# Attention with a KV cache and a gMLP branch on one core: picking heads by one product, a four-tile last wo group, and w_out's rest in 14, 10 and 8 rows

## The chip, the cores and the metric

The kernel runs on one core of one Trainium2 chip. The metric is the time of one run on the device in microseconds; I quote medians of several runs. In the profile PE is TensorE (PEld its weight loads), DVE is VectorE, ACT ScalarE, POOL GpSimd and SP SyncE; L458 is line 458 of the kernel concerned. The granted clock is the speed that TensorE was allowed, 1.00 being full speed. A load has landed when its last byte has arrived.

## The reference

Four tokens, one per batch, with 32 heads of 128 and caches of 4096 positions; the result has the shape (4, 1, 640).

```python
def reference(A_x, A_k_cache, A_v_cache, A_wq, A_wo, B_x, B_w_in, B_w_sp, B_b_sp, B_w_out):
    def _A_ref(x, k_cache, v_cache, wq, wo):      # B, Sq, D = 4, 1, 640; H, Dh = 32, 128
        q = (x @ wq).reshape(B, Sq, H, Dh).transpose(0, 2, 1, 3)
        scores = einsum('bhqd,bhkd->bhqk', q, k_cache) * Dh ** (-0.5)
        o = einsum('bhqk,bhkd->bhqd', softmax(scores), v_cache)
        return o.transpose(0, 2, 1, 3).reshape(B, Sq, H * Dh) @ wo
    def _B_ref(x, w_in, w_sp, b_sp, w_out):       # w_out: 864 x 640
        ...                                       # gelu, layernorm, gate, product with w_out
    xn = _layernorm(A_x)
    return A_x + _A_ref(xn, A_k_cache, A_v_cache, A_wq, A_wo) + _B_ref(xn, B_w_in, B_w_sp, B_b_sp, B_w_out)
```

## The kernel before

The caches are almost all of the 282.25 MB that are loaded. The heads are treated in four groups of eight (`NG = 4`, `HG = 8`), each in four units of K and of V, one per batch. A unit of V gives O (128 partitions x 4 x 128) in PSUM; four masked VectorE instructions make `R[:, b]` of it. When the four batches of a group are there, `emit_sel` picks each head's row (into `om`), `emit_oT` turns the result (into `oT`), and `emit_proj` multiplies it by the group's rows of wo. `o_bf` is the final sum, which is stored. Only for the last group is nothing left to load behind which this could be done.

```python
    # early: the last 96 rows of w_out, as 32 partitions of 3 rows (3840 bytes each), between w_out and K
    w_rest_d = B_w_out[nf:Fh, :].rearrange("(i r c) n -> r i c n", r=4, c=FR)
    for r in range(4):
        nc.sync.dma_start(out=w_rest[r:32:4], in_=w_rest_d[r])
    ...
    def emit_sel(g):
        oh = misc_ps([G, Dh], F32)                      # G = 32 rows: 8 heads x 4 batches
        for b in range(B):
            nc.tensor.matmul(oh[:], lhsT=SelR[:, b].rearrange("p h b -> p (h b)"), rhs=state["R"][:, b, :],
                             start=(b == 0), stop=(b == B - 1))
        om = ppool.tile([G, HG, Dh], BF16, tag="p", name="om")
        nc.vector.scalar_tensor_tensor(out=om[:], in0=oh[:, None, :].to_broadcast((G, HG, Dh)), ...)
    ...
    emit_proj(NG - 3)                                   # the tail, after V's last unit
    emit_sel(NG - 1)
    emit_proj(NG - 2, range(0, 4))
    emit_oT(NG - 1)
    emit_proj(NG - 2, range(4, HG))

    o_1 = ppool.tile([64, NO2], F32, tag="p", name="o_1")
    nc.vector.tensor_tensor(out=o_1[:], in0=proj[0:64, 0:NO2], in1=x_res[:], op=ALU.add)
    nc.vector.tensor_tensor(out=o_1[:], in0=proj[64:128, 0:NO2], in1=o_1[:], op=ALU.add)
    last = ps_l.tile([64, NO2], F32)
    oT = state[("oT", NG - 1)]
    for c in range(HG):
        lhsT = oT[:].rearrange("p c b -> p (c b)") if c == 0 else oT[:, c, :]
        for hf in range(NH):                            # two column tiles
            nc.tensor.matmul(last[32 * hf:32 * hf + (32 if c == 0 else B), :], lhsT=lhsT,
                             rhs=wo_t[NG - 1][:, c, hf * NO2:(hf + 1) * NO2], start=(c == 0), stop=(c == HG - 1))
    o_bf = ppool.tile([64, NO2], BF16, tag="p", name="o_bf")
    nc.vector.tensor_tensor(out=o_bf[:], in0=last[:], in1=o_1[:], op=ALU.add)
```

Of the kernel before, what the change touches and what calls it, by code (L numbers as in the profile page):

```python
# [9 lines left out]
ALU = mybir.AluOpType  # L10
AX = mybir.AxisListType
F32 = mybir.dt.float32
BF16 = mybir.dt.bfloat16
# [3 lines left out]
def kernel(  # L17
# [19 lines left out]
    nc = tc.nc  # L37
    P = 128
    B, Sq, D = A_x.shape
    _, H, Sk, Dh = A_k_cache.shape  # L40
    assert Sq == 1 and B == 4 and Dh == P and D % P == 0
    DC = D // P
    HG = 8
# [8 lines left out]
    NG = H // HG  # L52
    NU = NG * B
    G = HG * B
    F2 = B_w_in.shape[1]
    Fh = F2 // 2
    FA = 6
    FR = (Fh - FA * P) // 32
# [4 lines left out]
    NO2 = NOUT // NH  # L63
# [3 lines left out]
    const = ctx.enter_context(tc.tile_pool(name="const", bufs=1))  # L67
    small = ctx.enter_context(tc.tile_pool(name="small", bufs=2))
# [8 lines left out]
    ps_l = ctx.enter_context(tc.tile_pool(name="ps_l", bufs=1, space=bass.MemoryType.PSUM))  # L77
# [3 lines left out]
    def misc_ps(shape, dtype):  # L81
        misc_ctr[0] += 1
        return ps_m.tile(shape, dtype, tag="misc", name=f"misc{misc_ctr[0]}")
# [5 lines left out]
    def at_slot(i, n, off=0):  # L89
        return kv[:, i * SL + off:i * SL + off + n]  # L90
# [24 lines left out]
    nf = FA * P  # L115
# [3 lines left out]
    w_rest = w_rest_t[:32].bitcast(BF16)[:, 0:FR * NOUT].rearrange("p (c n) -> p c n", c=FR)  # L119

    NB = 32 * FC
    z_at = n_in + FA * NOUT
    w_rest_d = B_w_out[nf:Fh, :].rearrange("(i r c) n -> r i c n", r=4, c=FR)
    for r in range(4):
        nc.sync.dma_start(out=w_rest[r:32:4], in_=w_rest_d[r])  # L125


    seq = [("k", u) for u in range(B)]
# [36 lines left out]
    wo_t = [at_slot((4, 0, 1, 2)[g], HG * NOUT).rearrange("p (c n) -> p c n", c=HG) for g in range(NG)]  # L165
# [61 lines left out]
    SelH = const.tile([P, HG], F32)  # L227
    nc.vector.tensor_reduce(out=SelH[:], in_=I32[:].rearrange("p (h c) -> p h c", c=4), axis=AX.X, op=ALU.add)
    Mk4 = const.tile([P, 4], F32)
    nc.vector.tensor_reduce(out=Mk4[:], in_=I32[:].rearrange("p (h c) -> p c h", c=4), axis=AX.X, op=ALU.add)  # L230
    SelR = const.tile([P, B, HG, B], F32)
    nc.gpsimd.memset(SelR[:].rearrange("p x h b -> p (x h b)"), 0.0)
    for b in range(B):
        nc.vector.tensor_copy(out=SelR[:, b, :, b], in_=SelH[:])

    MkE = const.tile([P, NE], F32)
    nc.vector.tensor_reduce(out=MkE[:], in_=I32[:].rearrange("p (e m) -> p e m", e=NE), axis=AX.X, op=ALU.add)
# [8 lines left out]
    B32f = const.tile([G, B], F32)  # L246
# [17 lines left out]
    for hf in range(2):  # L264
        for c in range(DC):
            for j in range(NG):
                n0 = j * HG * Dh + hf * 512
                nc.tensor.matmul(q4_ps[32 * j:32 * j + 32, hf * 512:hf * 512 + 512], lhsT=xnT[:, c, :],  # L268
                                 rhs=wq[:, c, n0:n0 + 512], start=(c == 0), stop=(c == DC - 1))
# [4 lines left out]
    for a in range(2):  # L274
        op = nc.vector.tensor_copy if a == 0 else nc.scalar.copy
# [13 lines left out]
    for c in range(DC):  # L289
        for q in range(4):  # L290
# [29 lines left out]
                                   op0=ALU.mult, op1=ALU.subtract)  # L320
# [14 lines left out]
    for fc in range(FC):  # L335
        n = P if fc < FA else 32
        nb = B if fc > 1 else 32
        r0 = 64 * (fc % 2)
        for hf in range(NH):
            nc.tensor.matmul(proj[r0 + 32 * hf:r0 + 32 * hf + nb, 0:NO2], lhsT=uT[:n, fc, 0:nb],  # L340
                             rhs=(w_out[:, fc] if fc < FA else w_rest[:, fc - FA])[:, hf * NO2:(hf + 1) * NO2], start=(fc < 2), stop=False)
# [9 lines left out]
    state = {}  # L351
# [104 lines left out]

    def emit_sel(g):

        oh = misc_ps([G, Dh], F32)
        for b in range(B):  # L460
            nc.tensor.matmul(oh[:], lhsT=SelR[:, b].rearrange("p h b -> p (h b)"), rhs=state["R"][:, b, :],  # L461
                             start=(b == 0), stop=(b == B - 1))
        om = ppool.tile([G, HG, Dh], BF16, tag="p", name="om")
        nc.vector.scalar_tensor_tensor(out=om[:], in0=oh[:, None, :].to_broadcast((G, HG, Dh)),  # L464
                                       scalar=state.pop(("rinv", g))[:, 0:1],
                                       in1=MkH[:, :, None].to_broadcast((G, HG, Dh)), op0=ALU.mult, op1=ALU.mult)
        state[("om", g)] = om

    def emit_oT(g):
        om = state.pop(("om", g))[:].rearrange("p h (q c) -> p c h q", c=HG)  # L470
        oT_ps = misc_ps([P, HG, B], F32)
        for c in range(HG):
            nc.tensor.matmul(oT_ps[:, c, :], lhsT=om[:, c, :, :], rhs=B32[:], start=True, stop=True)
        oT = small.tile([P, HG, B], BF16, tag="oT", bufs=3)
        nc.vector.tensor_copy(out=oT[:], in_=oT_ps[:])
        state[("oT", g)] = oT

    def emit_proj(g, cs=range(HG)):
# [9 lines left out]
    for i, item in enumerate(seq):  # L488
# [13 lines left out]
        g, b = divmod(u, B)  # L502
        if key == "k":
            done = b == B - 1 and g > 0
            for k in range(8):
                emit_K(u, k)
                if done and k == 1:
                    emit_sel(g - 1)
                if done and k == 2:
                    emit_oT(g - 1)  # L510
                if done and k == 5 and g == 1:
                    emit_proj(g - 1)
            if b == B - 1:
                if g < NG - 1:
                    fill_qz(g + 1)
                softmax(g)
        else:
            emit_V(u)
    emit_proj(NG - 3)
# [5 lines that stand above are left out]
    o_1 = ppool.tile([64, NO2], F32, tag="p", name="o_1")  # L525
    nc.vector.tensor_tensor(out=o_1[:], in0=proj[0:64, 0:NO2], in1=x_res[:], op=ALU.add)
    nc.vector.tensor_tensor(out=o_1[:], in0=proj[64:128, 0:NO2], in1=o_1[:], op=ALU.add)
    last = ps_l.tile([64, NO2], F32)
    oT = state[("oT", NG - 1)]
    for c in range(HG):  # L530

        lhsT = oT[:].rearrange("p c b -> p (c b)") if c == 0 else oT[:, c, :]
        for hf in range(NH):
            nc.tensor.matmul(last[32 * hf:32 * hf + (32 if c == 0 else B), :], lhsT=lhsT,  # L534
                             rhs=wo_t[NG - 1][:, c, hf * NO2:(hf + 1) * NO2], start=(c == 0), stop=(c == HG - 1))

    o_bf = ppool.tile([64, NO2], BF16, tag="p", name="o_bf")
    nc.vector.tensor_tensor(out=o_bf[:], in0=last[:], in1=o_1[:], op=ALU.add)
    nc.sync.dma_start(out=out_flat[:, 0:NO2], in_=o_bf[0:B, :])
    nc.scalar.dma_start(out=out_flat[:, NO2:NOUT], in_=o_bf[32:32 + B, :])  # L540
# [28 lines left out]
```

## Time and profile before

| | before |
|---|---|
| median of the first three runs | 664.79 us (664.62 to 665.85) |
| span of the profiled run | 663.0 us |
| V's last unit landed, first and second part | 645.02, 649.92 |
| R of the last batch complete | 653.18 |
| oT of the last group cast | 655.89 |
| last wo group landed, first and last of four pieces | 657.63, 659.25 |
| o_bf done, output stored until | 660.54, 663.0 |

Read the table from its last row upwards. The output needs o_bf, o_bf needs the last wo group's products, and these need two things: oT, which descends from R, and the pieces of wo. The prediction below shows the chain of waits and the timeline from which the rows come. The view by stretches gives start, end and length of a stretch in us, then the busy time and count of PE, PEld, DVE, ACT and POOL, then the granted clock, the DMA share and GB/s. In the kernel before, for the last products and the final sums:

```profile
657.70:660.60 2.90, 2.27 (x16) 1.07 (x15) 0.71 (x2) 0.00 (x0) 0.00 (x0) 0.51 0.07 26
```

The clock was at half speed there (0.51), the DMA engines had nearly nothing left to do (0.07), and VectorE executed two instructions.

### The profile page before, as it was taken

Reading aid. Unit: us, or ns where it says so; the run is one execution under the profiler, and the core shown is the slowest. Engines: PE = TensorE matmul, PEld = TensorE weight load, DVE = VectorE, ACT = ScalarE, POOL = GpSimd, SP = SyncE. Lnnn points to the kernel's source line nnn. Section 1 sums busy time; section 2 is a strip of 40 time slices with the busy share of each in tenths; the row PEclk is TensorE's granted clock in tenths of the full one; section 3 lists DMA queues with packets and bytes.
Section 4 is the critical chain, followed back from the end, with each engine's and each line's share of the span. In section 5 each row is a group of like instructions: output and inputs, shape, how many; then the busy total and the mean of one; then the engine's idle time right before and its main releaser. Section 6 shows DMA issues by size and latency. Waiting matters only on the chain.

```text
span 663.0 us, 5426 instructions
## 1 busy us (share of the span) xinstructions
PE 289.5 (44%) x2283; PEld 106.4 (16%) x2283; DVE 362.0 (55%) x339; ACT 79.5 (12%) x163; POOL 10.7 (2%) x34
## 2 busy tenths in 40 slices
PE   0525765166072455235436075433506244634245
PEld 0101221022021122111112022110202112111112
DVE  4338999656190749609255286745619084960002
ACT  1200000541100000530200000070100000053200
POOL 3000000000000000000000000000000000000000
PEclk9758779678577677767858577865958769767677
DMA  9999999999999999999999999999999999999996
GB/s 370 463 440 428 407 438 441 439 428 436 428 435 432 431 415 446 431 435 436 427 439 436 427 416 446 437 439 428 415 440 439 436 439 406 453 420 433 429 416 253
DMA packets 6901, 282.61 MB, mean 426 GB/s; under 512 B 808, under 2 KB 1084, under 8 KB 1500
## 3 DMA queue, kind: packets, MB, share of 16 engines
q1 hardware_dynamic: 6856, 282.25, 98.8%
q8 instruction: 18, 0.29, 0.2%
q14 instruction: 7, 0.06, 0.0%
q10 hardware_dynamic: 20, 0.01, 0.0%
HBM read 282.25 MB, written 0.01 MB: 426 GB/s over the span
## 4 chain that ended last, share of the span: by engine, by line
DMA 74%; DVE 11%; issue 11%; PE 2%; ACT 1%; SPq 0%; DVEq 0%; ACTq 0%
DMA kv<-in_A_k_cache_dram 64%; DVE kT L361 11%; DMA kv<-in_A_v_cache_dram 4%; DMA kv<-in_A_wo_dram 3%; DMA kv<-in_A_wq_dram 2%; PE O L444 2%; ACT xd L426 0%; ACT Zb L407 0%; PE last L534 0%; PE S L372 0%; ACT p L415 0%; DVE pT L419 0%; DVE m L379 0%; PE misc L384 0%; SPq L125 0%
## 5 line engine op out<-in xcount | busy, mean ns | idle before, releaser
L361 DVE STREAM_TRANSPOSE kT<-kv 128x2048 f32<-128x2048 f32 x128 | 282.8, 2276 | 132.1 <-DMA kv<-in_A_k_cache_dram 132.1
L372 PE MATMUL S<-kT,QZ 128*32 128x512 bf16 x1024 | 188.3, 500 | 239.0 <-DVE kT L361 239.0
L372 PEld LDWEIGHTS <-QZ 128*32 128x32 bf16 x1024 | 60.6, 111 | 361.5 <-issue 341.0
L444 PE MATMUL O<-kv,Zb 128*32 128x512 bf16 x1024 | 74.6, 457 | 57.0 <-DMA kv<-in_A_v_cache_dram 36.7
L451 DVE TENSOR_SCALAR R<-O,Mk 128x128 f32<-128x128 f32 x16 | 5.6, 351 | 120.5 <-PE O L444 120.5
L407 ACT ACTIVATE Zb<-xd,MkE 32x256 bf16<-32x256 bf16 x116 | 53.0, 498 | 108.9 <-PE O L444 107.5
L444 PEld LDWEIGHTS <-Zb 128*32 128x32 bf16 x1024 | 33.4, 112 | 97.0 <-issue 55.7
L415 ACT ACTIVATE p<-S,negmax 128x512 bf16<-128x512 f32 x8 | 5.4, 683 | 312.3 <-DVE negmax L393 312.3
L461 PE MATMUL misc<-R,SelR 128*32 128x128 f32 x32 | 6.4, 281 | 26.2 <-DVE R L453 26.2
L453 DVE SCALAR_TENSOR_TENSOR R<-O,Mk,R 128x128 f32<-128x128 f32 x48 | 16.8, 351 | 1.7
L426 DVE COPY xd<-pT 32x256 bf16<-32x256 bf16 x44 | 16.1, 366 | 0.8
L426 ACT COPY xd<-pT 32x256 bf16<-32x256 bf16 x20 | 12.3, 613 | 5.6 <-DVE pT L419 5.2
L415 ACT ACT_TABLE_LOAD x1 | 1.3, 1283 | 92.7 <-DVE negmax L393 92.7
L347 POOL COPY QZ<-qT 32x32 bf16<-32x32 bf16 x16 | 5.1, 319 | 412.5 <-PE S L372 399.3
L419 DVE STREAM_TRANSPOSE pT<-p 128x1024 bf16<-128x1024 bf16 x4 | 5.0, 1246 | 7.6 <-ACT p L415 7.6
L379 DVE TENSOR_REDUCE m<-S 128x2 f32<-128x1024 f32 x4 | 4.9, 1225 | 5.4 <-PE S L372 5.4
L461 PEld LDWEIGHTS misc<-R,SelR 128*32 128x32 f32 x32 | 2.2, 107 | 34.0 <-DVE R L453 25.3
L268 PE MATMUL q<-kv,xnT 128*32 128x512 bf16 x40 | 4.0, 578 | 5.2 <-DMA kv<-in_A_wq_dram 5.2
L464 DVE SCALAR_TENSOR_TENSOR om<-misc,rinv,MkH 32x1024 bf16<-32x1024 f32 x4 | 5.1, 1272 | 2.0 <-PE misc L461 2.0
L430 PE MATMUL misc<-rowsum,SelP 128*32 128x2 f32 x8 | 1.1, 203 | 11.3 <-ACT p L415 11.3
L384 PE MATMUL misc<-dg,ones_f 128*128 128x256 f32 x8 | 2.7, 420 | 7.5 <-DVE dg L381 7.5
L276 DVE CAST kv<-q 128x512 bf16<-128x512 f32 x1 | 0.7, 692 | 9.1 <-PE q L268 9.1
(99 smaller groups left out, 72.5 us busy)
## 6 DMA issues: line engine op xcount, KB each, us to landing
kv<-in_A_k_cache_dram SPq DMA_DIRECT2D x8, 4096.0 KB
kv<-in_A_v_cache_dram SPq DMA_DIRECT2D x1, 6144.0 KB
kv<-in_A_wq_dram SPq DMA_DIRECT2D x1, 5120.0 KB
kv<-in_A_wo_dram SPq DMA_DIRECT2D x3, 1280.0 KB
kv<-in_B_w_in_dram SPq DMA_DIRECT2D x1, 2160.0 KB, 19.9
kv<-in_A_v_cache_dram SPq DMA_DIRECT2D x1, 2048.0 KB
kv<-in_B_w_out_dram SPq DMA_DIRECT2D x1, 960.0 KB
kv<-in_A_wo_dram SPq DMA_DIRECT2D x1, 640.0 KB, 22.5
```

What stands on the lines that cost most here:

```text
L347: nc.gpsimd.tensor_copy(out=QZ[r0:r0 + 32, :, :, :, 8 + 8 * hp], in_=qT[32 * g:32 * g + 32, NE * hp:NE * hp + NE].rearrange("p e a b -> p ...
L361: nc.vector.transpose(kT[:].rearrange("p (t r) -> p t r", r=32), kw)
L372: nc.tensor.matmul(S_ps[32 * q:32 * q + 32, e], lhsT=QZ[:, b, 2 * kh + w, e, w0:w0 + 32], rhs=kb[:, i, :, e, :, w], start=(b == 0 and k < ...
L407: nc.scalar.activation(out=dst, in_=src, func=ACT.Copy, scale=mk)
L415: nc.scalar.activation(out=p_bf[:, :, e, :], in_=S_ps[:, e], func=ACT.Exp, bias=negmax[:, e:e + 1], scale=scale, accum_out=rowsum[:, e:e + 1])
L419: nc.vector.transpose(pT[:].rearrange("p t h x -> p (t h x)"), p_bf[:].rearrange("p t e m -> p (t e m)"))
L426: op(out=xd[32 * hp:32 * hp + 32, :, q, :], in_=pT[32 * q:32 * q + 32, :, hp, :].rearrange("p t x -> p x t"))
L444: nc.tensor.matmul(O_ps[32 * q:32 * q + 32, :, :], lhsT=Zb[b % 2][:, w].rearrange("p h c -> p (h c)"), rhs=vv[:, w * 4 * Dh:(w + 1) * 4 * ...
L451: nc.vector.tensor_scalar(out=R, in0=O_ps[:, 0, :], scalar1=Mk4[:, 0:1], scalar2=None, op0=ALU.mult)
L453: nc.vector.scalar_tensor_tensor(out=R, in0=O_ps[:, c, :], scalar=Mk4[:, c:c + 1], in1=R, op0=ALU.mult, op1=ALU.add)
L461: nc.tensor.matmul(oh[:], lhsT=SelR[:, b].rearrange("p h b -> p (h b)"), rhs=state["R"][:, b, :], start=(b == 0), stop=(b == B - 1))
L464: nc.vector.scalar_tensor_tensor(out=om[:], in0=oh[:, None, :].to_broadcast((G, HG, Dh)), scalar=state.pop(("rinv", g))[:, 0:1], in1=MkH[: ...
```

## The change

Its intent is to take TensorE work out of the head picking (one float32 product instead of four), to spread the last wo group over four column tiles (products whose outputs start at partition 0, 32, 64 and 96 of PSUM; in the profile of before 16 products of the third group on four tiles take 0.71 us, the last group's 16 on two take 2.29 at half clock), and to even out the bytes among the DMA engines. I call the three parts **pick**, **tiles** and **rows**. In pick, the one product (with the mask `SelH4` in place of `SelR`) gives each of the 32 rows the values of all four batches, and four masked VectorE instructions keep those of the row's own batch, as `ob`. The diff, cut to its core:

```diff
-    w_rest_d = B_w_out[nf:Fh, :].rearrange("(i r c) n -> r i c n", r=4, c=FR)
-    for r in range(4):
-        nc.sync.dma_start(out=w_rest[r:32:4], in_=w_rest_d[r])
+    w_rest_d = B_w_out[nf:Fh, :].rearrange("(p c) n -> p c n", c=FR)
+    for r0, r1 in ((0, 14), (14, 24), (24, 32)):
+        nc.sync.dma_start(out=w_rest[r0:r1], in_=w_rest_d[r0:r1])
 ...
-        oh = misc_ps([G, Dh], F32)
-        for b in range(B):
-            nc.tensor.matmul(oh[:], lhsT=SelR[:, b].rearrange("p h b -> p (h b)"), rhs=state["R"][:, b, :], ...)
+        oh = misc_ps([G, B, Dh], F32)
+        nc.tensor.matmul(oh[:].rearrange("p b d -> p (b d)"), lhsT=SelH4[:].rearrange("p h b -> p (h b)"),
+                         rhs=state["R"][:].rearrange("p b d -> p (b d)"), start=True, stop=True)
+        ob = small.tile([G, Dh], F32, tag="ob", bufs=1)
+        nc.vector.tensor_scalar(out=ob[:], in0=oh[:, 0, :], scalar1=B32f[:, 0:1], scalar2=None, op0=ALU.mult)
+        for b in range(1, B):
+            nc.vector.scalar_tensor_tensor(out=ob[:], in0=oh[:, b, :], scalar=B32f[:, b:b + 1], in1=ob[:], op0=ALU.mult, op1=ALU.add)
 ...   # om reads ob instead of oh; oT gets one more chunk, set to zero for the last group
-    last = ps_l.tile([64, NO2], F32)
+    last_a = ps_l.tile([64, NO2], F32)
+    last_b = misc_ps([P, NO2], F32)
+    last = [last_a, last_b[64:128]]
+    part = {1: 1, 3: 1, 5: 1}
+    seen = set()
     for c in range(HG):
+        p = part.get(c, 0)
 ...   # chunk c goes to last[p]; the first product of each part is 32 columns wide
+        if c == 5:
+            nc.vector.tensor_tensor(out=o_1[:], in0=last[1], in1=o_1[:], op=ALU.add)
```

More of the change, by code (lines that the diff above doesn't have):

```diff
@@ L230 @@
     nc.vector.tensor_reduce(out=Mk4[:], in_=I32[:].rearrange("p (h c) -> p c h", c=4), axis=AX.X, op=ALU.add)
-    SelR = const.tile([P, B, HG, B], F32)
-    nc.gpsimd.memset(SelR[:].rearrange("p x h b -> p (x h b)"), 0.0)
-    for b in range(B):
-        nc.vector.tensor_copy(out=SelR[:, b, :, b], in_=SelH[:])
+    SelH4 = const.tile([P, HG, B], F32)
+    nc.vector.tensor_copy(out=SelH4[:], in_=SelH[:, :, None].to_broadcast((P, HG, B)))
     MkE = const.tile([P, NE], F32)
@@ L457, in emit_sel @@
     def emit_sel(g):
-        oh = misc_ps([G, Dh], F32)
-        for b in range(B):
-            nc.tensor.matmul(oh[:], lhsT=SelR[:, b].rearrange("p h b -> p (h b)"), rhs=state["R"][:, b, :],
-                             start=(b == 0), stop=(b == B - 1))
+        oh = misc_ps([G, B, Dh], F32)
[5 more added lines that the diff above has]
+            nc.vector.scalar_tensor_tensor(out=ob[:], in0=oh[:, b, :], scalar=B32f[:, b:b + 1], in1=ob[:], op0=ALU.mult, op1=ALU.add)
         om = ppool.tile([G, HG, Dh], BF16, tag="p", name="om")
-        nc.vector.scalar_tensor_tensor(out=om[:], in0=oh[:, None, :].to_broadcast((G, HG, Dh)),
+        nc.vector.scalar_tensor_tensor(out=om[:], in0=ob[:, None, :].to_broadcast((G, HG, Dh)),
                                        scalar=state.pop(("rinv", g))[:, 0:1],
@@ L473, in emit_oT @@
             nc.tensor.matmul(oT_ps[:, c, :], lhsT=om[:, c, :, :], rhs=B32[:], start=True, stop=True)
-        oT = small.tile([P, HG, B], BF16, tag="oT", bufs=3)
-        nc.vector.tensor_copy(out=oT[:], in_=oT_ps[:])
+        oT = small.tile([P, HG + 1, B], BF16, tag="oT", bufs=3)
+        nc.vector.tensor_copy(out=oT[:, 0:HG, :], in_=oT_ps[:])
+        if g == NG - 1:
+            nc.gpsimd.memset(oT[:, HG, :], 0.0)
         state[("oT", g)] = oT
@@ L527 @@
     nc.vector.tensor_tensor(out=o_1[:], in0=proj[64:128, 0:NO2], in1=o_1[:], op=ALU.add)
-    last = ps_l.tile([64, NO2], F32)
+    last_a = ps_l.tile([64, NO2], F32)
+    last_b = misc_ps([P, NO2], F32)
+    last = [last_a, last_b[64:128]]
     oT = state[("oT", NG - 1)]
+    part = {1: 1, 3: 1, 5: 1}
+    seen = set()
     for c in range(HG):
-        lhsT = oT[:].rearrange("p c b -> p (c b)") if c == 0 else oT[:, c, :]
+        p = part.get(c, 0)
+        lhsT = oT[:, c, :] if p in seen else oT[:, c:c + HG, :].rearrange("p c b -> p (c b)")
+        nb = B if p in seen else 32
         for hf in range(NH):
-            nc.tensor.matmul(last[32 * hf:32 * hf + (32 if c == 0 else B), :], lhsT=lhsT,
-                             rhs=wo_t[NG - 1][:, c, hf * NO2:(hf + 1) * NO2], start=(c == 0), stop=(c == HG - 1))
+            nc.tensor.matmul(last[p][32 * hf:32 * hf + nb, :], lhsT=lhsT,
+                             rhs=wo_t[NG - 1][:, c, hf * NO2:(hf + 1) * NO2], start=p not in seen, stop=c in (5, HG - 1))
+        seen.add(p)
+        if c == 5:
+            nc.vector.tensor_tensor(out=o_1[:], in0=last[1], in1=o_1[:], op=ALU.add)
     o_bf = ppool.tile([64, NO2], BF16, tag="p", name="o_bf")
-    nc.vector.tensor_tensor(out=o_bf[:], in0=last[:], in1=o_1[:], op=ALU.add)
+    nc.vector.tensor_tensor(out=o_bf[:], in0=last[0][:], in1=o_1[:], op=ALU.add)
     nc.sync.dma_start(out=out_flat[:, 0:NO2], in_=o_bf[0:B, :])
```

## The prediction

> **What bounds the kernel now.** I read the page first, then the chain of waits in order of time, then the timeline of the last 30 us, and then the groups by tile for the operations that the change touches. The page says that the DMA engines are busy in every slice:
>
> ```profile
> span 663.0 us, 5426 instructions
> ...
> DMA  9999999999999999999999999999999999999996
> ...
> q1 hardware_dynamic: 6856, 282.25, 98.8%
> ```
>
> The 282.25 MB at the 426 GB/s of the page fill the span; of TensorE (44%), VectorE (55%) and ScalarE (12%) none is near its limit. So nothing done between the first load and the last one shortens the run unless it takes bytes away or evens them out among the 16 engines. The only other place is the end, where the last loads have landed and something still has to be computed. The chain of waits shows it:
>
> ```profile
> 635.17 22.47 DMA kv<-in_A_wo_dram
> 657.63 0.04 issue
> 657.67 2.30 PE last L534 x16
> 659.98 0.04 DVEq L538
> 660.01 0.04 issue
> 660.06 0.48 DVE o_bf L538
> ```
>
> The load that releases the 16 last products lands at 657.63; they take 2.30 us; one VectorE add takes 0.48; from 660.54 to 663.0 the output is stored. The trace's landings say more: the four pieces of the last wo group land at 657.63, 658.43, 658.85 and 659.25. The products start at 657.67, 267 ns apart in each of two column tiles, so they finish behind the last landing: this tail is limited by TensorE, by some 0.3 us beyond what the loads would allow.
>
> A second path runs up to the same point, and the change lengthens it. The timeline, columns start, length, engine, line, operation, and in brackets the idle time before it:
>
> ```profile
> 652.06 1.12 DVE L453 SCALAR_TENSOR_TENSOR R<-O,Mk,R 128x128 f32<-128x128 f32 x3
> ...
> 653.37 0.27 PE L461 MATMUL misc<-R,SelR 128*32 128x128 f32 x1
> 653.38 0.80 PE L483 MATMUL proj<-kv,oT 128*4 128x320 bf16 x13
> 653.68 1.27 DVE L464 SCALAR_TENSOR_TENSOR om<-misc,rinv,MkH 32x1024 bf16<-32x1024 f32 x1 [0.50 <-PE misc L461]
> ...
> 655.01 0.66 PE L473 MATMUL misc<-B,om 32*128 32x4 bf16 x8 [0.82 <-DVE om L464]
> ...
> 655.70 0.19 DVE L475 CAST oT<-misc 128x32 bf16<-128x32 f32 x1 [0.75 <-PE misc L473]
> 656.14 0.71 PE L483 MATMUL proj<-kv,oT 128*4 128x320 bf16 x16 [0.48 <-DMA kv<-in_A_wo_dram]
> ```
>
> R is complete at 653.18, oT at 655.89. The last products need oT and wo's first piece of 657.63. So this path has **1.7 us of slack**, no more.
>
> [...] the granted clock is 1.00 from 653.0 to 656.6 and 0.50 from 658 to 660; 320 columns are 135 ns apart in the first stretch and 267 ns in the second. [...] L483 on four tiles starts 3 to 4 ns apart, 16 products in 0.71 us, while L534 on two tiles takes 2.29 us for 16 (at half clock). [...] the trace has 351 ns for L453, and the trace's figure is used below. [...] the four loads of 8 rows all go to engines 0 to 7, and 14, 10 and 8 rows go to 14, 10 and 8 engines. The trace agrees: the first two show 8 data landings each.
>
> **The change, part by part.**
>
> *w_out's rest.* One row of 3840 B took 149 ns in the packet records. Before, engines 0 to 7 carry four rows, 0.6 us more than the others. After, they carry three, engines 8 and 9 two, 10 to 13 one, 14 and 15 none. Engines 0 to 7 gain one row, 0.15 us; 8 to 13 lose 0.15 to 0.30. But the last landings are not spread by these rows alone: the fastest engine finishes the last wo piece at 654.80, the slowest at 659.25, and the 18 instruction fetches (16 KB, about 1 us each on their queue, then a stretched data packet, some 1.46 us of an engine's time) make most of that. Of the three engines that end last, I could follow one to w_out's rows and one not. So the loads end between 0.15 us earlier and 0.2 later: about zero.
>
> *Heads picked by one product.* Removed: four float32 products of 128 columns a group (32 records, two passes each, 281 ns mean). Only batch 3's is on the last path: 653.18 to 653.68, the rest ran earlier as each R came. Added: one product of 512 columns, which can start only when all four R are there. A pass of 128 columns was 109 ns from start to start when undisturbed, so 512 columns take four times that[...]; the last pass of 256 columns lasted 379 ns, [...] so one of 512 lasts 0.59. Start 653.24 + 0.43 + 0.59 = 654.25. Then four VectorE instructions of 32x128 from PSUM, each like L451 and L453: 351 ns, 386 from start to start. From 654.29: 3 x 386 + 351 gives 655.80. Then om, 1.27 us from 655.84 to 657.11; the 8 products of L473's kind from 657.16, 0.66 us; the cast at 657.86 to **658.05, 2.16 us later than before**. The slack was 1.7.
>
> In the three earlier groups the same 2.2 us of VectorE and some 0.5 us of TensorE fall where VectorE waits for the next K unit (132.1 us idle before L361 on the page): free.
>
> *Order on TensorE.* In the changed program the 16 products of the third wo group (656.14 before) stand behind the 8 of om, so they now start about 657.87 and not at 656.14. At full clock they are through at 658.57, at half clock at 659.14. VectorE's sums follow: o_1 twice, now a third addition for the second part, then o_bf: four instructions of 0.48, 0.52 apart.
>
> *Last wo group on four tiles.* Eight rounds of products become five (chunks 0/1, 2/3, 4/5, 6, 7): at half clock 5 x 267 = 1.34 us and not 2.13, so 0.8 us less TensorE time. The memset of the padding on GpSimd comes behind the cast, a tenth of a microsecond, before it is needed.
>
> *Sum.* At half clock: L483's kind ends 659.14, the last products start at 658.94; part two ends 659.94; o_1 is done at 660.18, its third addition at 660.70, o_bf at 660.74 to 661.22: 0.68 later than 660.54. At full clock: proj done 658.57, o_1 659.61, part two 658.98, but the last piece of wo lands at 659.25, its products end at 659.6; third addition 659.65 to 660.13, o_bf to 660.65: 0.11 later. I take 0.45 as the middle, leaning to half clock[...]. 664.79 + 0.45 = 665.2.
>
> **The rivals.** (a) *The four tiles win*: the pick's added time is overestimated, say the masked sums take 250 ns or L483's products are not held back; then the 0.8 us saved leave the last landing as the bound, products to 659.6, and the run is about 664.4. For it: the tail before was bound by TensorE. Against: the added instructions form one dependent line and none can be overlapped, and the durations of their kind vary by 2 ns only. (b) *The loads decide*: if the late engines are among 0 to 7, all landings come 0.15 us earlier, V's last unit too, 664.6 to 664.7; if they are among 8 to 13, up to 0.3 later, 665.5 with the rest. For it: the DMA row; against: the fetches dominate the spread. (c) *The clock*: a warm tail would make it 664.9, a cold one throughout, om's products included, 665.7.
>
> **Range and chances.** The estimates run from 664.4 to 665.9; three runs of before spread from 664.62 to 665.85, which is as large as the whole effect. So 665.2, from 664.4 to 666.1. Two per cent are 13 us, twenty times what any part can do: within 2% has 0.98, the other two 0.01 each.
>
> **What would show it.** In the changed profile: one float32 product of 128x512 in two passes, about 0.43 apart; four VectorE instructions of about 0.35 in a row after R; the cast of oT some 2.1 us later after R than 2.7 us before; the third group's 16 products after om's 8, no longer waiting for a DMA; the chain at the end running over VectorE (R, ob, om) and not over the wo load, with o_bf starting under 0.1 us after o_1's third addition at half clock. It is wrong if the chain still comes from the wo load and the last products end before 659.7, or if the last landing moves by over 0.3 us.

Passages are cut, with the cuts marked. The sum: 664.79 + 0.45 = 665.2. Two of its inputs can be had from the trace of the kernel before: 0.43 us is four times the 108 to 109 ns between two undisturbed passes of 128 columns (432 to 436 ns), and 0.59 is the 379 ns of a pass of 256 columns plus twice 108 (595 ns). The place of 0.45 between 0.11 and 0.68, and that the fetches make most of the spread of the landings, were estimates.

The traces number no DMA engines; 0 to 15 are names for them. What the traces show is the count. In the kernel before, each of the four loads of w_out's rest lands in 8 pieces, and the 32 rows run in eight lines of four, 151 to 152 ns from start to start. In the changed kernel the three loads land in 14, 10 and 8 pieces, and the rows run in eight lines of three, two of two and four of one. So the counts that were forecast came true.

## The result

The changed kernel is correct and takes **665.87 us** (median of six runs, 665.35 to 667.48); the kernel before took 664.80 in six runs of the same rounds (664.62 to 665.85). The ratio is 1.0015, with a 95% interval from 1.0002 to 1.0028. Ratios here are the mean time of one kernel's fast runs over that of the other's of the same rounds, so not quite the ratio of the medians that I quote. The change costs about a microsecond, and its runs scatter over 2.1 us.

These lines of the page of the changed kernel answer to those of before:

```profile
span 664.1 us, 5392 instructions
...
DMA  9999999999999999999999999999999999999995
...
q1 hardware_dynamic: 6856, 282.25, 98.7%
```

The bytes and packets are the same, and the engines are as busy. What changed lies in the tail. The end of the chain of waits (start, length, what):

```profile
636.20 23.11 DMA kv<-in_A_wo_dram
659.31 0.49 DVE o L530
...
659.82 0.50 DVE o L531
...
660.42 0.50 DVE o L548
...
661.04 0.48 DVE o_bf L551
```

Before, the load of wo released 16 products and one addition. Now four additions in a row end the run. The label of the first row misleads: L530 is put down to a wo load, but it needs the third group's products of L487, which the timeline of the changed kernel shows (start, length, engine, line, operation, in brackets the idle time before it and its releaser):

```profile
652.35 1.13 DVE L451 SCALAR_TENSOR_TENSOR R<-O,Mk,R 128x128 f32<-128x128 f32 x3
653.53 0.62 PE L458 MATMUL misc<-R,SelH 128*32 128x512 f32 x1 [1.62 <-DVE R L451]
...
653.98 0.59 PE L458 MATMUL misc<-R,SelH 128*32 128x512 f32 x1
...
654.61 0.34 DVE L461 TENSOR_SCALAR ob<-misc,B32f 32x128 f32<-32x128 f32 x1 [1.14 <-PE misc L458]
654.99 1.08 DVE L463 SCALAR_TENSOR_TENSOR ob<-misc,B32f,ob 32x128 f32<-32x128 f32 x3
656.11 1.27 DVE L466 SCALAR_TENSOR_TENSOR om<-ob,rinv,MkH 32x1024 bf16<-32x1024 f32 x1
...
658.01 1.24 PE L487 MATMUL proj<-kv,oT 128*4 128x320 bf16 x16
658.12 0.19 DVE L477 CAST oT<-misc 128x32 bf16<-128x32 f32 x1 [0.74 <-PE misc L475]
```

One line of dependent work leads from R (653.47) through the product, the four masked sums and om to the cast at 658.31. The first piece of the last wo group had landed at 658.10, so this line is now the later of the two inputs, by 0.2 us. L487's last 16 products (L483 in the kernel before, where they ran at 656.14 in 0.71 us) stand behind om's on TensorE, start at 658.01 and take 1.24 us. The same stretch as in the section on before:

```profile
657.70:660.60 2.90, 2.87 (x39) 1.34 (x37) 1.35 (x4) 0.00 (x0) 0.00 (x0) 0.53 0.09 35
```

TensorE, which executed 16 matmuls here before, executes 39 at half clock (0.53) and is busy in 2.87 of 2.90 us.

From R to the end of o_bf the changed kernel takes 8.05 us (653.47 to 661.52) and the kernel before 7.36 (653.18 to 660.54): 0.69 more. The spans differ by 1.09. The rest is R, 0.29 later, and the store of the output, 0.11 longer. The landings in the tail all come 0.47 later (V's last unit 645.49 after 645.02, the last wo piece 659.72 after 659.25). The prediction had no reason for that much: its rival (b) allowed up to 0.3.

### The profile page after: what moved, and what is told of

Same layout as the page of the kernel before. It is cut to its first block, busy times and chain, and to the rows that moved or that the text cites. A ratio compares the mean times of both kernels' runs of the same rounds, so it can differ in the third digit from the quotient of the medians.

```text
span 664.1 us, 5392 instructions
## 1 busy us (share of the span) xinstructions
PE 286.5 (43%) x2259; PEld 103.6 (16%) x2259; DVE 367.7 (55%) x353; ACT 79.5 (12%) x163; POOL 10.6 (2%) x34
## 4 chain that ended last, share of the span: by engine, by line
DMA 74%; DVE 12%; issue 11%; PE 2%; ACT 1%; SPq 0%; DVEq 0%; ACTq 0%
DMA kv<-in_A_k_cache_dram 63%; DVE kT L359 11%; DMA kv<-in_A_v_cache_dram 4%; DMA kv<-in_A_wo_dram 3%; DMA kv<-in_A_wq_dram 2%; PE O L442 2%; ACT xd L424 0%; ACT Zb L405 0%; PE S L370 0%; ACT p L413 0%; DVE pT L417 0%; DVE m L377 0%; SPq L169 0%; PE misc L382 0%; DVE o L548 0%
## 5 line engine op out<-in xcount | busy, mean ns | idle before, releaser
L475 PE MATMUL misc<-B,om 32*128 32x4 bf16 x32 | 2.6, 199 | 10.9 <-DVE om L466 10.9
L458 PE MATMUL misc<-R,SelH 128*32 128x512 f32 x8 | 4.2, 604 | 6.5 <-DVE R L451 6.5
L487 PE MATMUL proj<-kv,oT 128*4 128x320 bf16 x48 | 5.2, 402 | 0.0
```

What stands on the lines that cost most here:

```text
L487: nc.tensor.matmul(proj[r0:r0 + B, 0:NO2], lhsT=oT[:, c, :], rhs=wo_t[g][:, c, hf * NO2:(hf + 1) * NO2], start=False, stop=(g == NG - 2 an ...
```

## The experiments

Twelve kernels ran, five times each, in three sets. Each set had nine runs of the kernel before on its own chip, with medians of 664.89, 664.72 and 664.88; the table lists the sets in this order, four kernels each. All are correct but two that load wrong rows on purpose. "vs before" is the difference of the medians within the set.

| kernel | median (range), us | vs before | ratio, 95% interval |
|---|---|---|---|
| pick_alone | 665.66 (664.36 to 666.17) | +0.77 | 1.0007, 0.9994 to 1.0019 |
| tiles_alone | 664.54 (664.36 to 664.63) | -0.35 | 0.9992, 0.9980 to 1.0005 |
| rows_alone | 665.48 (665.09 to 665.63) | +0.59 | 1.0006, 0.9994 to 1.0019 |
| rows_tiles | 665.21 (664.95 to 665.34) | +0.32 | 1.0004, 0.9990 to 1.0017 |
| rows_blocks | 665.25 (665.09 to 665.66) | +0.53 | 1.0009, 0.9995 to 1.0022 |
| rows_16 | 665.41 (665.19 to 665.59) | +0.69 | 1.0008, 0.9996 to 1.0021 |
| after_order | 664.94 (664.76 to 665.01) | +0.22 | 1.0001, 0.9989 to 1.0014 |
| after_warm | 664.91 (664.83 to 665.11) | +0.19 | 1.0002, 0.9989 to 1.0014 |
| rows_src | 665.07 (664.41 to 665.39) | +0.19 | 1.0000, 0.9988 to 1.0013 |
| rows_dst | 665.21 (665.05 to 666.22) | +0.33 | 1.0006, 0.9993 to 1.0018 |
| pick_tiles | 664.64 (664.51 to 665.55) | -0.24 | 0.9998, 0.9985 to 1.0010 |
| tiles_warm | 664.58 (664.35 to 665.04) | -0.30 | 0.9995, 0.9982 to 1.0009 |

Every one of these intervals holds 1, so no single row is proof of a gain or a loss. What carries the argument is that rows agree with each other and with times read from the traces. The table of those (us, profiled run of each):

| kernel | R | oT cast | last wo landing | o_bf done | R to oT | R to o_bf |
|---|---|---|---|---|---|---|
| before | 653.18 | 655.89 | 659.25 | 660.54 | 2.71 | 7.36 |
| changed | 653.47 | 658.31 | 659.72 | 661.52 | 4.84 | 8.05 |
| pick_alone | 653.10 | 657.95 | 659.17 | 661.59 | 4.85 | 8.49 |
| tiles_alone | 652.55 | 655.26 | 659.23 | 660.29 | 2.71 | 7.74 |
| pick_tiles | 652.66 | 657.51 | 659.33 | 660.38 | 4.85 | 7.72 |
| rows_alone | 653.29 | 655.99 | 659.99 | 661.30 | 2.70 | 8.01 |
| rows_tiles | 653.58 | 656.30 | 659.80 | 660.85 | 2.72 | 7.27 |
| after_order | 653.06 | 658.14 | 659.73 | 660.79 | 5.08 | 7.73 |
| after_warm | 653.29 | 658.13 | 659.97 | 660.89 | 4.84 | 7.60 |
| tiles_warm | 652.50 | 656.48 | 659.17 | 660.09 | 3.98 | 7.59 |

### One part alone: pick_alone, tiles_alone, rows_alone, rows_tiles

*pick_alone* has these hunks of the change and the old last group:

```diff
-        for b in range(B):
-            nc.tensor.matmul(oh[:], lhsT=SelR[:, b]..., rhs=state["R"][:, b, :], ...)
+        nc.tensor.matmul(oh..., lhsT=SelH4..., rhs=state["R"][:].rearrange("p b d -> p (b d)"), start=True, stop=True)
+        ...   # ob by four masked sums; om reads ob
```

> The kernel before with the pick of the heads alone (one product, four masked sums). Theory 1 (the pick is the cost: it puts 2.1 us between R and oT, of which 1.7 us were slack, and holds the 16 products of the third wo group back): R to oT's cast end takes 4.85 us instead of 2.71, the last products start at about R + 5.8 us and go on in eight rounds of two tiles, o_bf ends 1.2 to 1.3 us later after R than before at half clock, time about 666.0, ratio 1.0018. Theory 2 (the loads' rows make the difference): ratio 1.000, within 0.15 us of before.

Measured: 665.66, +0.77. R to oT takes 4.85 us instead of 2.71, just as in the changed kernel, and R to o_bf 8.49 instead of 7.36, 1.13 more; expected were 1.2 to 1.3. The five runs scatter over 1.8 us, the widest of the twelve; the profiled one is the slowest.

*tiles_alone*:

```diff
-    last = ps_l.tile([64, NO2], F32)
+    last = [last_a, last_b[64:128]]
+        ...   # chunks 1, 3, 5 to the second part; third addition at c == 5; oT padded
```

> The kernel before with the last wo group on four column tiles and two parts alone. Theory 1 (this part saves TensorE time, but the last landing of wo comes right behind): the products end at about 659.76 instead of 659.96 with the last landing at 659.25, the third addition lies before the end of the products, o_bf ends 0.2 to 0.3 us earlier, time 664.5, ratio 0.9996. Rival (the third addition and the memset cost more than the rounds save): time 664.9 to 665.3 and o_bf waiting for o_1.

Measured: 664.54, -0.35; its five runs lie below all nine of before. Its chain of waits ends so:

```profile
658.46 0.43 PE last_a L542 x2
...
658.90 0.82 PE last_a L542 x4
...
659.80 0.48 DVE o_bf L549
```

The products end 0.5 us behind the last landing (659.23) and not 0.7 as before, and o_bf starts at 659.80: the four tiles do what they are for.

*rows_alone* and *rows_tiles* (with the hunks of tiles_alone):

```diff
-    w_rest_d = B_w_out[nf:Fh, :].rearrange("(i r c) n -> r i c n", r=4, c=FR)
-    for r in range(4):
-        nc.sync.dma_start(out=w_rest[r:32:4], in_=w_rest_d[r])
+    w_rest_d = B_w_out[nf:Fh, :].rearrange("(p c) n -> p c n", c=FR)
+    for r0, r1 in ((0, 14), (14, 24), (24, 32)):
+        nc.sync.dma_start(out=w_rest[r0:r1], in_=w_rest_d[r0:r1])
```

> The kernel before with the loads of w_out's rest by 14, 10 and 8 rows alone. Theory 1: the tail from R on stays at 7.36 us to the end of o_bf, and the time moves by no more than 0.3 us either way. Theory 2 (in the changed kernel the last unit of V landed 0.47 us later than before, and every engine's first K packet was stretched by 0.28 us at 22.5 us, which is this part's doing): the same stretched packets here, V's last unit lands at 645.3 to 645.6 instead of 645.02, time 665.1 to 665.3.

> The change without its pick. Theory 1: all of the loss goes with the pick, 664.3 to 664.9, at least 0.8 us below the changed kernel's 665.87. Theory 2 (the rows cost): 665.2 or more.

Measured: 665.48 alone (+0.59) and 665.21 on top of tiles_alone's 664.54 (+0.67). The five runs of rows_tiles (664.95 to 665.34) all lie above the five of tiles_alone (664.36 to 664.63) of the same set. So about the same cost came twice, from a part whose intent was to balance the engines. It sits in the loads. The expected 7.36 us from R to o_bf became 8.01 in rows_alone, because o_bf follows the landing of wo, 0.74 later than before, and not R, 0.11 later. First the line of V's last products in the timeline of the kernel before, then in that of rows_alone; the start is the landing of V's first part plus about 0.14:

```profile
645.16 6.46 PE L444 MATMUL O<-kv,Zb 128*32 128x512 bf16 x64 [7.29 <-DMA kv<-in_A_v_cache_dram]
```

```profile
645.89 4.21 PE L444 MATMUL O<-kv,Zb 128*32 128x512 bf16 x48 [7.28 <-DMA kv<-in_A_v_cache_dram]
```

V's last unit lands 0.73 us later (645.75 after 645.02), 14 us before the last landing. So the delay was not made at the end of the run; it came earlier.

### Where the rows' time is lost: rows_blocks, rows_16, rows_src, rows_dst

The packet records show where. Near 22.5 us, when w_out's rest is loaded and the first unit of K (64-KB rows) begins behind it, all 16 of the first K packets take 2418 ns in the kernel before. In the changed kernel they take 2506 to 2855. The view by stretches over those two microseconds, for before and then for the changed kernel:

```profile
22.00:24.00 2.00, 2.00 (x19) 0.64 (x12) 0.89 (x2) 0.00 (x0) 0.82 (x3) 1.00 1.43 611
```

```profile
22.00:24.00 2.00, 2.00 (x19) 0.64 (x12) 0.91 (x2) 0.00 (x0) 0.80 (x3) 1.00 1.59 615
```

The packets that start there (a packet counts where it starts, so the share can exceed 1) took 1.59 instead of 1.43 of the engines' time for nearly the same bytes. I call this the pause. It could come from the uneven counts 14/10/8, from the neighbouring rows read in HBM, or from the neighbouring partitions written. Four kernels separate these; all are edits of the kernel before.

```diff
 rows_blocks: four loads of 8 neighbouring partitions, 8 neighbouring source rows each
+    ...   # w_rest_d by "(p c) n -> p c n", as in the change
+        nc.sync.dma_start(out=w_rest[8 * r:8 * r + 8], in_=w_rest_d[8 * r:8 * r + 8])
 rows_16: two loads of 16, to every second partition
+    ...   # w_rest_d by "(i r c) n -> r i c n" with r=2
+    for r in range(2):
+        nc.sync.dma_start(out=w_rest[r:32:2], in_=w_rest_d[r])
 rows_src: neighbouring source rows, still to every fourth partition (wrong result on purpose)
-    w_rest_d = B_w_out[nf:Fh, :].rearrange("(i r c) n -> r i c n", r=4, c=FR)
+    w_rest_d = B_w_out[nf:Fh, :].rearrange("(r i c) n -> r i c n", r=4, c=FR)
 rows_dst: the old source rows, to neighbouring partitions (wrong result on purpose)
-        nc.sync.dma_start(out=w_rest[r:32:4], in_=w_rest_d[r])
+        nc.sync.dma_start(out=w_rest[8 * r:8 * r + 8], in_=w_rest_d[r])
```

> The kernel before, still four loads of 8 rows for w_out's rest, but each into 8 neighbouring partitions instead of every fourth one. No engine carries more or less than before. Theory P (neighbouring partitions make the pause that all 16 engines showed at 22.5 us in every profile with the new rows, and in none without): the first K packets are stretched by 0.2 to 0.4 us here too and the last wo piece lands at 659.5 to 659.6, time +0.3 us. Theory Q (the uneven engine counts of 14 and 10 make it): no stretched packet over 0.1 us, last landing 659.25, time as before.

> The kernel before with w_out's rest in two loads of 16 rows, every second partition: two rows on each of the 16 engines, so engines 8 to 15 carry 0.30 us more and 0 to 7 0.30 us less. If the engine that ends last is among 8 to 15 (as 0.2 to 0.4 us of the rows run beyond its pause suggest): last landing 659.5 to 659.6, time +0.3 us with no pause. If it is among 0 to 7: last landing 658.95, time -0.2 to -0.3. If the pause comes from more than 8 engines at once on these rows: stretched packets here too.

> Wrong result on purpose: four loads of 8 rows, each into every fourth partition as in the kernel before, but from 8 neighbouring rows of w_out. If the pause belongs to the side that is written (several engines at once in one group of neighbouring partitions): no stretched K packet, time as before, 664.7 to 664.9. If it belongs to the side that is read (several engines at once in one stretch of w_out): stretched by 0.2 to 0.4 us, time 665.2 to 665.5.

> Wrong result on purpose, the other half: four loads of 8 rows into 8 neighbouring partitions, from every fourth row of w_out as before. Written side: stretched packets and 665.2 to 665.5. Read side: none, 664.7 to 664.9. If both this and the other show the pause, either alone is enough; if neither does, it takes both.

How many engines these four kernels use was the author's estimate, extended from the 8, 14 and 10 pieces in which loads of 8, 14 and 10 rows land in the profiles of the kernel before and the changed one.

From the packet records of all fourteen profiles (the lengthening is the excess over 2418 ns of the first 16 K packets):

| partitions written by one load | profiles | w_out rows over 149 ns, of 32 | lengthening, median ns |
|---|---|---|---|
| every fourth, 8 rows | before, pick_alone, tiles_alone, pick_tiles, tiles_warm, rows_src | none in any | 0 in all six |
| 14, 10, 8 neighbours | changed, rows_alone, rows_tiles, after_order, after_warm | 2 to 5, up to 312 ns | 231 to 357 |
| 8 neighbours | rows_blocks, rows_dst | 7 and 5, up to 331 ns | 264, 389 |
| every second, 16 rows | rows_16 | 2, up to 182 ns | 334 |

The split is complete: eight of eight against none of six. rows_blocks has the pause with four loads of 8 rows, as before, so 14/10/8 is not needed for it. rows_src has neighbouring source rows and no pause, and rows_dst has the old source rows and the pause, so **it belongs to the partitions written**. The same two microseconds as above, for rows_src and then for rows_dst:

```profile
22.00:24.00 2.00, 2.00 (x22) 0.66 (x15) 1.40 (x2) 0.00 (x0) 0.38 (x2) 1.00 1.37 584
```

```profile
22.00:24.00 2.00, 2.00 (x19) 0.65 (x12) 1.23 (x2) 0.00 (x0) 0.54 (x2) 1.00 1.64 611
```

rows_src takes engine time in proportion to its bytes, as the kernel before does (1.37 for 584, 1.43 for 611); rows_dst takes 1.64 for the same 611. The landing of V's last unit points the same way, but less clearly. In the timeline of rows_src and then of rows_dst:

```profile
645.42 4.08 PE L444 MATMUL O<-kv,Zb 128*32 128x512 bf16 x48 [7.13 <-DMA kv<-in_A_v_cache_dram]
```

```profile
645.92 4.63 PE L444 MATMUL O<-kv,Zb 128*32 128x512 bf16 x48 [6.79 <-DMA kv<-in_A_v_cache_dram]
```

In the six profiles without the pause it lands at 644.94 to 645.28, in the eight with it at 645.36 to 645.89, but rows_blocks (645.36) is only 0.08 behind rows_src. The medians 665.07 and 665.21 are too close to decide, and rows_src's 665.07 lies above the 664.7 to 664.9 expected without a pause.

The packet records also show why the end of the run is a poor place to measure this. Near 111 us, the mean end of the 64-KB packets of the first unit of V is 0.31 to 0.60 us later than in the kernel before in the eight profiles with the pause, and between 0.02 earlier and 0.03 later in the others. Between 130 and 150 us (from the second group's first unit of K to the second unit of V) several profiles then shift against the kernel before by up to 0.4 us, with the pause or without it, and the two groups overlap from there on (0.16 to 0.46, and -0.07 to 0.39). No run here shows what causes that shift.

Why the partitions written make the pause, and why it holds up all of the first 16 K packets (2506 to 2855 ns in the changed kernel), the runs do not show. What is shown is the split in the table.

Part of the rows' cost also stays open. The last landing is at 659.84 on average in the five profiles with 14/10/8 and at 659.28 in the six without a pause, 0.56 later; the pause in those five is 0.29 on average. The other 0.27 would fit the two more rows on two engines that the prediction named (0.30, two rows of 149 ns). But rows_dst and rows_blocks, both with the pause and four loads of 8 rows as before, land at 660.00 and 659.57, and rows_src, with neither, at 659.52. Landings of equal arrangement differ by up to 0.35, so single profiles cannot settle it.

### The clock and the order in the tail: after_warm, after_order

Both are edits of the changed kernel. after_warm puts 16 idle products (nobody reads their results) between the picking product and om's, so that TensorE stays busy. after_order executes the third group's 16 products before om's.

```diff
 after_warm
+    behind = tc.issue_after(picked.ins)
+    with behind:
+        for i in range(16):
+            busy = nc.tensor.matmul(last_a[0:32, :], lhsT=ident_bf[:, 0:32], rhs=Zb[0]...[:, 0:NO2], start=True, stop=True)
+    with tc.issue_after(busy.ins):
+        emit_proj(NG - 2, range(0, 4))
+        emit_oT(NG - 1)
 after_order
-    emit_proj(NG - 2, range(0, 4))
-    emit_oT(NG - 1)
-    emit_proj(NG - 2, range(4, HG))
+    ahead = emit_proj(NG - 2)
+    with tc.issue_after(ahead.ins):
+        emit_oT(NG - 1)
```

> The changed kernel with 16 idle products of 320 columns behind the pick, so that TensorE is busy while VectorE sums and its clock should stay up. The result is unchanged. Theory 1 (half clock in the tail costs 0.57 us by the prediction's two sums): the products of the third and last group are 135 ns apart instead of 267, o_bf ends 0.5 to 0.8 us earlier, time 665.1 to 665.4, with a smaller spread. If the clock falls all the same or doesn't matter: 665.9.

> The changed kernel with the 16 products of the third wo group tied ahead of om's 8 products. Theory 1 (holding them back is what puts VectorE's sums at the end): they run at 656.2 to 656.9, o_1's first two additions are over before the last products, o_bf waits for the last products and ends 0.7 to 0.8 us earlier, time 665.0 to 665.2. Rival (oT's own lateness is what counts): o_bf ends at most 0.2 us earlier.

Measured: 664.91 and 664.94, against the changed kernel's 665.87 (other sets; relative to their own runs of before +0.19 and +0.22 against +1.07). The spread falls from 2.1 us to 0.28 and 0.25. In after_warm the stretch of the tail reads:

```profile
657.70:660.60 2.90, 2.06 (x36) 0.94 (x34) 1.85 (x5) 0.00 (x0) 0.00 (x0) 1.00 0.14 47
```

The clock is 1.00 and not 0.53; in the stretch before (654.50 to 657.70) TensorE was busy for 3.06 of 3.20 us, in the changed kernel for 0.88. In after_order it was mixed (0.71), but its chain of waits ends with products released by the wo load again, no longer with L530 and L531:

```profile
636.29 22.64 DMA kv<-in_A_wo_dram
...
658.97 0.43 PE last_a L545 x2
...
660.30 0.48 DVE o_bf L552
```

From the last landing to o_bf the changed kernel takes 1.80 us, after_warm 0.92 and after_order 1.06, although R to oT is no shorter in either. So in these profiles the line over VectorE delays the end where 16 products at half clock and two additions stand behind it. Either remedy puts the landing of wo back in charge. after_warm gained more than expected (665.1 to 665.4).

### Without the rows: pick_tiles, tiles_warm

*pick_tiles* has the hunks of pick_alone and tiles_alone. *tiles_warm* is tiles_alone with the 16 idle products of after_warm.

```diff
 tiles_warm, on top of tiles_alone
+    picked = emit_sel(NG - 1)
+    ...   # 16 products of 320 columns behind it, as in after_warm
```

> The change without its rows. By the prediction's sums (loads as before) 0.11 to 0.68 us later than before according to the clock, 0.45 in the middle: 664.9 to 665.5, median 665.2, no stretched packet, last landing near 659.25. If the pick costs more than worked out, 665.6 or more; if the rows' cost does not add, as the changed kernel's 665.87.

> The kernel before with the four tiles alone and 16 idle products behind the old pick, to keep the clock up in the tail: a version that might beat both. The last landing of wo stays at 659.23; the last products then end 0.30 us after it instead of 0.48, o_bf ends at 660.1, time 0.1 to 0.2 us below the four tiles alone: 664.3 to 664.4. If the clock falls all the same, 664.5.

Measured: 664.64 and 664.58. pick_tiles is the surprise: I expected it to cost, and it is 0.24 below before. Its chain of waits ends so:

```profile
635.99 22.52 DMA kv<-in_A_wo_dram
...
658.55 0.43 PE last_a L544 x2
...
659.90 0.48 DVE o_bf L551
```

Here the pick is hidden: R is complete at 652.66 and oT at 657.51, before wo's first piece (657.71), although R to oT takes 4.85 us, as in the changed kernel. V's last products ran partly at full clock, as the stretch of pick_tiles shows (clock 0.76):

```profile
645.50:651.00 5.50, 4.88 (x64) 1.98 (x56) 0.00 (x0) 0.00 (x0) 0.00 (x0) 0.76 0.98 414
```

In the kernel before they ran at half clock (0.51 in the same stretch), 64 products in 6.46 us, and R came half a microsecond later. So the slack is not a constant of the kernel. One of the five runs of pick_tiles took 665.55, which may be a run without that luck, but only one run was profiled.

In tiles_warm the last group's products start 0.14 us apart (657.61 and 657.75) and not 0.27 as at half clock, and the last landing to o_bf takes 0.92 us (659.17 to 660.09), in tiles_alone 1.06 (659.23 to 660.29). The 0.14 are not visible in the times: 664.58 is above the 664.3 to 664.4 that I expected. The two are the fastest kernels here, below both the kernel before and the changed one by their medians. Neither is shown faster than before: their intervals reach 1.0005 and 1.0009.

## Why the prediction was right or wrong

The predicted total, 665.2 within 664.4 to 666.1, holds the measured 665.87. That it does is partly luck: against the kernel before, 0.45 us more was predicted and 1.07 measured. The worst case of one term (half clock, 0.68) came true, and R came 0.29 later behind loads that landed 0.47 later; the range had room for both.

**The pick's line of work: right.** R to oT was worked out as 4.87 us (653.18 to 658.05) and measured as 4.84. The passes of 512 columns start 453 ns apart (0.43 us worked out), the last one took 590 as worked out, and the sums 339 ns each instead of 351.

**Order on TensorE: right.** The third group's products started at 658.01 (657.87 worked out, with R 0.29 earlier) and took 1.24 us at half clock. The chain runs over VectorE, with the additions 0.52 to 0.62 apart rather than 0.52; o_bf started 0.13 us after the third addition, where the prediction named under 0.1 as a sign. The printed chain does name the wo load, against another of its signs, by the misleading label above.

**The sum at half clock: right in size.** 0.68 us later was worked out, and R to o_bf grew by 0.69. after_warm and after_order show that it takes both the half clock and the order. Some side terms were wrong without effect. VectorE's busy time grew by 5.7 us in all (362.0 to 367.7), 1.4 a group and not 2.2, which is the length of the path. TensorE's fell by 3.0 us (289.5 to 286.5), where the prediction added 0.5 a group. The memset of the padding did not come behind the cast but ran at 428.3 us.

**The tiles: right in size.** The prediction took 0.8 us less TensorE time, of which the last landing leaves only what brings the products' end to about 659.6. In tiles_alone they end at 659.71, o_bf 0.25 earlier than before, and the median is 0.35 lower.

**w_out's rest: mis-sized.** This is the step that failed: "the loads end between 0.15 us earlier and 0.2 later: about zero". It measured +0.59 alone and +0.67 on top of the tiles. The redistribution of bytes was the wrong question, since rows_blocks keeps four loads of 8 rows and costs 0.53. What the step left out is which partitions the engines write at the same time: with the new partitions the first K packets took 231 to 357 ns longer (median by profile), and part of the cost beyond that stays open.

**The slack of 1.7 us: read from one run and taken for a constant.** R's end lay between 652.50 and 653.58 in the ten profiles of the table above, whereas wo's landing does not follow R. Where R came early, the pick was hidden (pick_tiles).

**The rivals.** Rival (a), the tiles win, is what pick_tiles did (664.64; "about 664.4"), for another reason than a cheaper pick. Rival (b) had loads up to 0.3 us later from balance; the landings did come 0.47 later, but the pause, which rows_blocks shows with four loads of 8 rows as before, already lengthened the first K packets by 0.28. Rival (c), the clock, is right for a warm tail: "664.9" was predicted and after_warm took 664.91, though with later loads than it assumed. The prediction's own test, the last landing moving by over 0.3 us, is met (0.47), so by its own terms its account of the loads is wrong, although the total lies in the range.

**What does not add up.** The single effects sum to 0.77 + 0.59 - 0.35 = 1.01, close to the change's 1.07. But pick_tiles (-0.24) and the rows (0.6) would give 0.36. Between pick_tiles and the changed kernel o_bf moved by 1.14: R came 0.81 later (the landing of V's second part 0.39 of it; the rest is put down to the clock of V's products, 0.50 against 0.76 from 645.50 to 651.00) and R to o_bf grew by 0.33 at half clock. Whether the later loads shift the clock against the work, or five and six runs drew differently, the runs do not settle.

## What to carry to other kernels

Before you change a small load within a saturated stream, ask which partitions its engines write at the same moment, not only how many bytes each carries; a stride that looks odd may be there for that (here the first 16 K packets took 231 to 389 ns longer behind neighbouring or every second partition, and 0 behind every fourth). When work is moved onto a dependent line beside the last loads, its cost is its length minus a slack that is not fixed (R ended at 653.18 with V's products at a clock of 0.51 and at 652.66 with them at 0.76), so read the slack from several profiles, and look at what stands behind the line on the same engine. Run each part alone: here, by the medians, one part helped, one cost, and one did either.

## What else these profiles show

- A small load in a saturated stream: when its rows went to neighbouring or every second partition, the first 16 K packets behind it took 231 to 389 ns longer (median by profile) in eight of eight profiles, 0 in six of six otherwise, and the medians of the runs rose by 0.3 to 0.7 us, single intervals all holding 1 (rows_src, without it, rose by 0.2).
- Two loads of 16 rows to every second partition (665.41) were no better than four of 8 to neighbours (665.25), and both medians were above that of four of 8 to every fourth (664.72).
- om of 32x1024 elements took 1272 ns with a source in PSUM (before) and 1273 with it in SBUF (changed). The short sums of 128 elements a partition from PSUM took 351 ns at 128 partitions and 339 at 32.
- A float32 product has two records in the trace, 8 for the four picking products. Those of 512 columns start 453 ns apart at full clock, so 1.77 ns for a column of a product, against 0.42 for a bf16 column (320 in 135 ns): four times the cost in two records.
- The kernel before has 18 instruction fetches of 16 KB, 0.99 to 1.11 us each on their queue, and 21 of its 3456 packets of 64 KB took 2541 to 3601 ns instead of 2418, 13 of them starting within 2 us of the start of a fetch.
